# A sliding-window attention and mixer kernel: its instruction order from a written-out list in place of a scheduler in the kernel, and loads and stores on two queues

## The chip, the cores and the metric

The kernel runs on one core of one Trainium2 chip. A core has five engines that run side by side: TensorE (PE) multiplies matrices into PSUM, VectorE (DVE), ScalarE (ACT) and GpSimd (POOL) work elementwise, and SyncE (SP) issues transfers. The metric is the device time in microseconds (us). A profile's span is the time from the first to the last event of the program in one profiled execution; it is a little shorter than the timed figure.

## The reference

Attention with a sliding window of 128 keys and 4 sink keys, over 4 batches, 8 heads, 768 positions, 64 dimensions a head; its output x (768 x 512 a batch) goes through a mixer:

```
scores = q @ k.T / sqrt(64);  keep = is_sink | in_window
a = softmax(where(keep, scores, -1e9));  x = a @ v
tok = w_tok @ (alpha1 * x + beta1)            # mixes the 768 positions
u   = x + lam * tok
out = u + lam * (relu((alpha2 * u + beta2) @ w_ch1) @ w_ch2)   # 512 -> 2048 -> 512
```

## The kernel before

Every batch passes the same stages. Positions are tiled by 128 (six row tiles), heads are taken in pairs, and matrix operands are fp16.

- **Attention.** q and k of a head pair are loaded (`load_qk`), cast to fp16 and transposed into `qkT` (`trans`; batches 0 and 1 on PE as `tp`, batches 2 and 3 by a DMA transpose on SP). `scores` makes `S` on PE, ACT takes the exponential into `E`, DVE or POOL masks it. `sinks` does the sink keys (`sk`, `es`), `fill_vs` their values (`vs`). `pv` multiplies `E` with v (`vfs`), and DVE divides by the row sum (`rec`, then `x`, L850 and L851). POOL and DVE make `xh` = lam * (alpha1 * x + beta1) from it (`tm` L869, `xh` L872).
- **Token mix** (`tok`, L956): six products of 512 columns a row tile with the transposed `w_tok` (`wtokT`, made by `cast_wtok` at the start); DVE adds the result to x (L963), ACT or POOL casts it to `u` in fp16 (L356, L358).
- **Transpose of u** into `uT`: in batch 0 on PE (`uTp`, L997), else by DMA transpose on SP (L1015). DVE or ACT apply alpha2 and beta2 (L982, L980).
- **Channel mix.** First layer `mlp1`: four products of 384 columns for each of 16 feature tiles and two halves of the positions (`h`, L1036), relu on ACT (L1042) or DVE (L1044). Second layer: in batch 0 directly (`ch`, L1221), in batches 1 to 3 by a Strassen scheme of seven products (`P`, L1153), for which DVE makes sums of `hT` (`h_sums`: S3 L1094, S1 L1095, S2 L1096, S4 L1097) and of the weights (`w2_sums`, L1068), and DVE or POOL add the partial results to x (L1166, L1184, L1189, L1192). The row tile is then stored.

All of this is a list of some 1140 tasks. Each is added by `add` with a priority, the engines that may run it with an assumed cost in ns, the tasks it waits for and the buffers it uses:

```
a = add(p, {PE: 4 * 161}, mm, [done["uT", b, chk, c] for c in range(NC)] + [done["w1", fi // 4]], [ph, bu])
done["h", b, chk, fi] = add(p + 0.1, {ACT: 493, DVE: 556}, relu, [a], [ph, bh])
```

`Plan.run` is a list scheduler that runs while the program is built: it keeps a clock for each engine, a model of the transfer queues (`Rings`), and the buffers of each kind that are free (`homes`), and takes the open task that could start first, ties by priority; the priorities are shuffled by 30 seeds (`TURNS`). A POOL task, and a DVE task with `port=True`, also waits for the other's end (`port`). What it picks fixes three things: the order of the instructions on every engine, the engine of a task that has a choice, and which buffer a tile lives in (a later tile in the same buffer waits for the readers of the earlier one). It also puts idle products (`idle`, L349, on the tile `warm`) where PE would wait in the first 36 us. On the chip the order is fixed and nothing is assumed: an engine takes its instructions in turn and waits on semaphores. PSUM has four banks of kind `d` (all products but the scores) and two double ones of kind `S`.

SP issues nearly all loads, DMA transposes and stores (`nc.sync.dma_start`); POOL issues the loads that cast (w_ch1, and q and k of batch 0 except the first pair); ACT issues five small ones at the start. Tiny loads (`gate`) hold SP until parts of w_ch1 have landed.

Of the kernel before, what the change touches and what calls it, by code (L numbers as in the profile page):

```python
# [10 lines left out]
FP16 = mybir.dt.float16  # L11
# [6 lines left out]
SEEN = {PE: 200, ACT: 60, DVE: 60, POOL: 70}  # L18


class Buf:


    def __init__(self, kind, shape, dtype, name):
        self.kind, self.shape, self.dtype, self.name = kind, shape, dtype, name
        self.left = 0
        self.freed = 0.0
        self.home = None
        self.t = None


FW = 1.0

SWDONE = 1800.0


class Rings:


    WIRE = {"hw": 1600.0, "sw": 2100.0}  # L40

    HOLDS = 128.0

    def __init__(self):
        self.now = 0.0
        self.queue = {"hw": [], "sw": []}
        self.given = {"hw": [], "sw": []}

    def issue(self, ring, t, at):
        self.given[ring].append(t)  # L50
        self.queue[ring].append([t, float(t.lands[0]), float(t.lands[1]), at + self.WIRE[ring]])

    def room(self, ring, lands, at):

        keep = self.now, {r: [list(h) for h in q] for r, q in self.queue.items()}
        self.step(at)
        g = self.given[ring]
        last = g[-8] if len(g) >= 8 and g[-8].seen is None else None
        q = self.queue[ring]
        while last is not None and any(h[0] is last for h in q):  # L60
            self.step(float("inf"))
        over = sum(h[1] for h in q) + lands[0] - self.HOLDS
        while ring == "hw" and over > 0 and q:
            if q[0][1] < over:
                self.step(float("inf"))
                over = sum(h[1] for h in q) + lands[0] - self.HOLDS
            else:
                self.now += over * q[0][2]
                over = 0
        to = max(at, self.now)  # L70
        self.now, self.queue = keep
        return to

    def step(self, until):

        while True:
            heads = [(r, q[0]) for r, q in self.queue.items() if q]
            if not heads:
                return None
            live = [(r, h) for r, h in heads if h[3] <= self.now]  # L80
            later = [h[3] for r, h in heads if h[3] > self.now]
            turn = sum(h[2] for r, h in live)
            ends = [(self.now + h[1] * turn, r) for r, h in live]
            end = min(ends) if ends else (float("inf"), None)
            to = min([end[0], until] + later)
            for r, h in live:
                h[1] -= (to - self.now) / turn
            self.now = to
            if end[0] <= to:
                return self.queue[end[1]].pop(0)[0]  # L90
            if to >= until:
                return None

    def peek(self):

        keep = self.now, {r: [list(h) for h in q] for r, q in self.queue.items()}
        t = self.step(float("inf"))
        at = self.now if t else float("inf")
        self.now, self.queue = keep
        return at  # L100
# [11 lines left out]
class Plan:  # L112
# [19 lines left out]
    def run(self, prio):  # L132

        tasks = self.tasks
        rank = [0] * len(tasks)
        for r, i in enumerate(sorted(range(len(tasks)), key=lambda i: (prio[i], i))):
            rank[i] = r
        waiting = [len(t.needs) for t in tasks]
        ready = [t.since for t in tasks]
        homes = {k: [0.0] * n for k, n in self.homes.items()}  # L140
        busy = {k: [False] * n for k, n in self.homes.items()}
        for t in tasks:
            t.seen = None
            for b in t.uses:
                b.left, b.freed, b.home = 0, 0.0, None
        for t in tasks:
            for b in t.uses:
                b.left += 1
        free = {PE: 0.0, ACT: 3500.0, DVE: 3200.0, POOL: 500.0, SP: 0.0}
        rings = Rings()  # L150
        open_ = []
        steps = []

        def end(t, seen):
            t.seen = seen
            for b in t.uses:
                b.left -= 1
                b.freed = max(b.freed, seen)
                if b.left == 0:
                    busy[b.kind][b.home] = False  # L160
                    homes[b.kind][b.home] = b.freed
            for o in t.then:
                ready[o.i] = max(ready[o.i], seen)
                waiting[o.i] -= 1
                if not waiting[o.i]:
                    bisect.insort(open_, (rank[o.i], o.i))

        def pick():
            best = None
            spare = {k: sorted(h for h, x in zip(homes[k], busy[k]) if not x) for k in homes}  # L170
            for r, i in open_:
                at = ready[i]
                if best is not None and at > best[0]:
                    continue
                t = tasks[i]
                asked = {}
                for b in t.uses:
                    if b.home is None:
                        asked[b.kind] = asked.get(b.kind, 0) + 1
                if any(len(spare[k]) < n for k, n in asked.items()):  # L180
                    continue
                at = max([at] + [spare[k][n - 1] for k, n in asked.items()])
                own = None
                for e in t.engs:
                    at_e = max(free[e], at)
                    if e == POOL or (e == DVE and t.port):
                        at_e = max(at_e, port)
                    key = (at_e + FW * t.engs[e], at_e, r, at_e + t.engs[e], i, e)
                    if own is None or key < own:
                        own = key  # L190
                if best is None or own[1:] < best:
                    best = own[1:]
            return best

        open_ = sorted((rank[t.i], t.i) for t in tasks if not waiting[t.i])
        mode = None
        port = 0.0
        landing = float("inf")
        until, _, took = self.fill
        while len(steps) < len(tasks):  # L200
            best = pick()
            if best is None or landing <= best[0]:
                assert landing < float("inf"), "no task can go on"
                t = rings.step(float("inf"))
                end(t, rings.now + (SWDONE if POOL in t.engs else 300.0))
                landing = rings.peek()
                continue
            start, r, _, i, e = best
            open_.pop(bisect.bisect_left(open_, (r, i)))
            t = tasks[i]  # L210
            for b in t.uses:
                if b.home is None:
                    b.home = min((h, n) for n, (h, x) in enumerate(zip(homes[b.kind], busy[b.kind]))
                                 if not x)[1]
                    busy[b.kind][b.home] = True
            idle = None
            n = int((start - max(free[PE], 400.0)) / (took if free[PE] > 4500.0 else 110.0))
            if e == PE and free[PE] < until and n > 0:
                spare = [(h, k) for k, (h, x) in enumerate(zip(homes["d"], busy["d"])) if not x]
                if spare and min(spare)[0] <= free[PE]:  # L220
                    idle = (min(spare)[1], n)
                    homes["d"][idle[0]] = start
                    mode = None
            cost = t.engs[e]
            if t.lands:
                cost += rings.room("sw" if e == POOL else "hw", t.lands, start) - start
            if e == PE:
                if start < 4500.0:
                    cost = cost * 2
                if t.mode != mode:  # L230
                    cost = cost + 95
                mode = t.mode
            free[e] = start + cost
            if e == POOL or (e == DVE and t.port):
                port = free[e]
            steps.append((t, e, start, free[e], idle))
            if t.lands:
                rings.step(start)
                rings.issue("sw" if e == POOL else "hw", t, free[e])
                landing = rings.peek()  # L240
            else:
                end(t, free[e] + SEEN[e])
# [1187 lines left out]
```

The softmax here doesn't subtract the row's maximum and nothing guards it: scores larger than these inputs give would overflow.

## Time and profile before

| | |
|---|---|
| time, median of 3 | 256.93 us (256.84 to 257.47) |
| span of the profiled execution | 255.3 us |
| PE, DVE, ACT, POOL busy | 247.4, 190.0, 142.6, 88.3 us |
| instructions on PE, DVE, ACT, POOL | 2174, 402, 236, 108 |
| first `tok` product starts | 30.35 us |
| last product starts, last store issued | about 251.9, 252.46 us |
| moved from and to HBM | 29.91 MB read, 6.29 MB written |

The profile lists groups of instructions by source line, engine and tile. In a timeline a row has the start, the length, the engine, the line, what is written from what, how many instructions follow each other, and in brackets how long the engine was idle before it and who released it. A PE row's length runs to the end of its last product, and products overlap, so their distance is read from start to start. A `q` behind an engine's name (SPq, ACTq) is its sequencer, which issues transfers.

### The profile page before, as it was taken

Reading aid. Unit: us, or ns where it says so; the run is one execution under the profiler, and the core shown is the slowest. Engines: PE = TensorE matmul, PEld = TensorE weight load, DVE = VectorE, ACT = ScalarE, POOL = GpSimd, SP = SyncE. Lnnn points to the kernel's source line nnn. Section 1 sums busy time; section 2 is a strip of 40 time slices with the busy share of each in tenths; the row PEclk is TensorE's granted clock in tenths of the full one; section 3 lists DMA queues with packets and bytes.
Section 4 is the critical chain, followed back from the end, with each engine's and each line's share of the span. In section 5 each row is a group of like instructions: output and inputs, shape, how many; then the busy total and the mean of one; then the engine's idle time right before and its main releaser. Section 6 shows DMA issues by size and latency. Waiting matters only on the chain.

```text
span 255.3 us, 5519 instructions
## 1 busy us (share of the span) xinstructions
PE 247.4 (97%) x2174; PEld 160.9 (63%) x2174; DVE 190.0 (74%) x402; ACT 142.6 (56%) x236; POOL 88.3 (35%) x108
## 2 busy tenths in 40 slices
PE   8999998999999999899999999999999999999994
PEld 7754645675555544456678676558668666667883
DVE  6777998696878878578889997877789764136782
ACT  2689845989848035688971225867571125775000
POOL 7409802344445330159653460735310101000000
PEclk9999999999999999999999999999999999999999
DMA  6998999999943998599778689501000156000105
GB/s 202 195 223 292 216 230 392 373 370 218 218 73 115 186 260 190 117 205 220 155 138 182 125 191 251 85 3 21 3 0 3 59 167 146 0 0 3 63 4 185
DMA packets 86130, 38.80 MB, mean 152 GB/s; under 512 B 73540, under 2 KB 80460, under 8 KB 86104
## 3 DMA queue, kind: packets, MB, share of 16 engines
q1 hardware_dynamic: 82320, 35.14, 56.5%
q0 software_dynamic: 3744, 3.28, 8.1%
q8 instruction: 17, 0.28, 0.5%
q14 instruction: 9, 0.07, 0.1%
q10 hardware_dynamic: 40, 0.03, 0.0%
HBM read 29.91 MB, written 6.29 MB: 142 GB/s over the span
## 4 chain that ended last, share of the span: by engine, by line
PE 88%; DMA 4%; DVE 3%; POOL 1%; issue 1%; ACT 1%; POOLq 0%; ACTq 0%
PE h L1036 33%; PE P L1153 21%; PE tok L956 11%; PE ch L1221 8%; PE pv L825 5%; PE S L724 4%; DMA n<-in_q_dram 4%; DVE uT L982 1%; PE S L719 1%; PE tp L614 1%; PE pv L818 1%; POOL n L497 1%; PE wT L916 1%; ACT uT L980 1%; DVE w2f L1068 1%
## 5 line engine op out<-in xcount | busy, mean ns | idle before, releaser
L1036 PE MATMUL h<-uT,w1f 128*128 128x384 f16 x512 | 91.9, 326 | 2.7 <-DVE uT L982 1.3
L1036 PEld LDWEIGHTS <-w1f 128*128 128x128 f16 x512 | 47.3, 98 | 34.5 <-issue 5.5
L1042 ACT ACTIVATE hT<-h 128x384 f16<-128x384 f32 x99 | 48.3, 492 | 26.1 <-PE h L1036 25.6
L1153 PEld LDWEIGHTS <-hT 128*128 128x128 f16 x408 | 39.8, 98 | 6.7
L746 ACT ACTIVATE E<-S 128x1024 f16<-128x1024 f32 (+1 forms) x39 | 37.9, 1001 | 7.5 <-PE S L724 3.7
L869 POOL TENSOR_TENSOR tm<-x,la_b 128x512 f32<-128x512 f32 x18 | 26.2, 1454 | 26.3 <-DVE xh L872 19.1
L956 PE MATMUL tok<-xh,wtokT 128*128 128x512 f16 x144 | 33.4, 379 | 0.0
L356 ACT CAST u<-x 128x512 f16<-128x512 f32 x19 | 11.7, 618 | 31.2 <-DVE x L963 31.1
L1153 PE MATMUL P<-w2f,hT 128*128 128x256 f16 x216 | 25.9, 273 | 0.0
L1166 DVE TENSOR_TENSOR x<-x,P 128x256 f32<-128x256 f32 x45 | 18.3, 418 | 8.2 <-PE P L1153 7.9
L1044 DVE TENSOR_SCALAR hT<-h 128x384 f16<-128x384 f32 x29 | 15.8, 553 | 10.9 <-PE h L1036 10.5
L956 PEld LDWEIGHTS <-wtokT 128*128 128x128 f16 x144 | 14.0, 98 | 14.6
L1221 PE MATMUL ch<-w2f,hT 128*128 128x512 f16 x96 | 23.0, 379 | 0.0
L1153 PE MATMUL P<-w2s,hT 128*128 128x256 f16 x192 | 22.8, 273 | 0.0
L851 DVE TENSOR_TENSOR x<-pv,rec 128x256 f32<-128x256 f32 x48 | 20.4, 424 | 1.7
L358 POOL CAST vfs<-vnat 128x512 f16<-128x512 f32 x18 | 15.0, 840 | 16.2 <-DMA vnat<-in_v_dram 16.0
L963 DVE TENSOR_TENSOR x<-x,tok 128x512 f32<-128x512 f32 x24 | 16.2, 684 | 5.7 <-PE tok L956 5.7
L356 ACT CAST n<-nat 128x768 f16<-128x768 f32 x16 | 13.2, 829 | 10.8 <-DMA nat<-in_q_dram 8.8
L825 PEld LDWEIGHTS <-E 128*128 128x128 f16 x328 | 15.2, 97 | 6.0 <-issue 1.6
L825 PE MATMUL pv<-vfs,E 128*128 128x65 f16 x328 | 17.9, 194 | 0.0
L358 POOL CAST u<-x 128x512 f16<-128x512 f32 x5 | 3.1, 621 | 34.8 <-DVE x L963 21.1
L1221 PEld LDWEIGHTS <-hT 128*128 128x128 f16 x96 | 8.6, 98 | 9.1 <-issue 0.2
(131 smaller groups left out, 327.4 us busy)
## 6 DMA issues: line engine op xcount, KB each, us to landing
out_dram<-x SPq DMA_DIRECT2D x21, 256.0 KB, 2.8
nat<-in_q_dram SPq DMA_DIRECT2D x13, 384.0 KB, 5.3
nat<-in_k_dram SPq DMA_DIRECT2D x13, 384.0 KB, 5.7
vnat<-in_v_dram SPq DMA_DIRECT2D x18, 256.0 KB, 5.2
wst_w<-in_moe_w_ch_dram SPq DMA_DIRECT2D x8, 512.0 KB, 7.4
wtn<-in_moe_w_tok_dram SPq DMA_DIRECT2D x6, 384.0 KB, 4.7
w1f<-in_moe_w_ch_dram POOLq DMA_DIRECT2D x4, 512.0 KB, 11.1
v<-in_v_dram SPq DMA_DIRECT2D x12, 128.0 KB, 6.4
```

The lines of the kernel that those rows point to most:

```text
L356: nc.scalar.copy(o, i)
L358: engine[e].tensor_copy(o, i)
L746: nc.scalar.activation(eT.t, pS.t[:, :, 0 : n * w].rearrange("p e (i w) -> p e i w", i=n), AF.Exp, scale=scale)
L825: nc.tensor.matmul(po.t[:, hl, :], eT.t[:, e_, off + i, c : c + P], vf[j][:, h, :], start=(r < 2 and n == 0), stop=(n == len(parts) - 1 an ...
L851: nc.vector.tensor_mul(bx.t[:, 4 * G : 4 * G + 4, :], po.t[:, :, 0:D], rec.t.to_broadcast([P, 4, D]))
L869: engine[e].tensor_mul(bt.t, bx.t.rearrange("p h d -> p (h d)"), la1_b)
L956: nc.tensor.matmul(pt.t, wtokT[:, si, ti * P : (ti + 1) * P], hs[si].t, start=(si == 0), stop=(si == NR - 1))
L1036: nc.tensor.matmul(ph.t, w1f[:, c, fi * P : (fi + 1) * P], bu.t[:, c, chk * NTOK : (chk + 1) * NTOK], start=(c == 0), stop=(c == NC - 1))
L1042: nc.scalar.activation(bh.t[:, fi, :], ph.t, AF.Relu)
L1153: nc.tensor.matmul(pc.t, hh[:, nt * P : (nt + 1) * P], w(fi), start=(first and n_ == 0), stop=(n_ == HF - 1), skip_group_check=True)
L1166: nc.vector.tensor_add(row(bx)[:, cols], row(bx)[:, cols], pc.t)
L1221: nc.tensor.matmul(pc.t, bh.t[:, fi, nt * P : (nt + 1) * P], w2f[:, fi, :], start=(fi == 0), stop=(fi == NF - 1))
```

## The change

The scheduler leaves the kernel. What it would choose is written out: `ORDER` (the tasks in the order of the program), `ENGINES` (the engine of each), `HOMES` (the buffer of each tile), `IDLES` (where idle products stand, and how many). They come from a search outside the kernel, over fixed orders, with other assumed costs (for an exponential 50 + 0.85 a column in place of 170 + 0.835, for a relu 395 on ACT and 480 on DVE in place of 493 and 556), and with the port of DVE and POOL given to whoever asked first. Loads of q, k, v, w_tok and w_ch2 and all stores of results may be issued from ACT as well as from SP; DMA transposes stay on SP. `gates` has a tile of its own.

```diff
-    def run(self, prio):
-        ...
-    def emit(self, turns):
-        prio = [t.prio for t in self.tasks]
-        for seed in turns:
-            prio = shuffle(prio, seed)
-        for t, e, start, stop, idle in self.run(prio):
-            t.at = (e, start, stop)
+    def emit(self, order, engines, homes, idles):
+        own = iter(homes)
+        for t in self.tasks:
+            for b in t.uses:
+                if b.home is None:
+                    b.home = int(next(own), 16)
+        fills = {i: (home, n) for i, home, n in idles}
+        for i in order:
+            t = self.tasks[i]
+            e = (ACT, DVE, PE, POOL, SP)[int(engines[i])]
+            idle = fills.get(i)
...
+    queue = {SP: nc.sync, ACT: nc.scalar}
...
-    gates = sb.tile([1, 32], FP16, tag="pt_1", bufs=1, name="gates")
+    gates = const.tile([1, 32], FP16, name="gates")
...
-    TURNS = (13523, 134113, ...)
+    ORDER = (26, 6, 9, 7, 11, 8, 10, 3, 18, 0, 1, 72, 19, 73, 15, ...)
+    ENGINES = ("3313134433443333444444444444444433334443131211211202021212021203030121211211211210200200" ...)
+    HOMES = ("23100237431101330030022023311032230023102103010110051014013521b0006220a41141110314003021" ...)
+    IDLES = ((73, 0, 44), (46, 0, 16), (49, 0, 26), (90, 2, 8), (61, 2, 1), (109, 3, 1), (68, 3, 1),
+        (111, 2, 2), (88, 2, 2), (166, 2, 2))
...
-            p, {SP: 550}, lambda e: nc.sync.dma_start(
+            p, {SP: 570, ACT: 560}, lambda e: queue[e].dma_start(
                 bf.t, v[b, :, r * P : (r + 1) * P, :].rearrange("h p d -> p h d")),
...
-            add(p, {SP: 480}, lambda e: nc.sync.dma_start(out[b, ti * P : (ti + 1) * P, cols], row(bx)[:, cols]),
+            add(p, {SP: 520, ACT: 550}, lambda e: queue[e].dma_start(out[b, ti * P : (ti + 1) * P, cols], row(bx)[:, cols]),
```

How many of each task stand on which engine, before and after (the others stay): relus on ACT 99 and 77, on DVE 29 and 51; casts of q and k on ACT 16 and 21, on POOL 8 and 3; products of w_ch2 with lam on DVE 15 and 8, on POOL 1 and 8; additions of lam * beta1 (`xh`) on DVE 17 and 13, on POOL 1 and 5; loads and stores issued by ACT behind its first five 0 and 36. The order on PE changes from end to end; the end of batch 0's token mix, for one, goes from `tok_4, tok_3, uTp, uTp, h` to `tok_4, tok_3, uTp, uTp, tok_5, h`, and idle products from 106 to 103.

## The prediction

> **What bounds the kernel now.** I read the page first: part 1 (busy time) and part 4 (the chain that ended last).
>
> ```profile
> span 255.3 us, 5519 instructions
> PE 247.4 (97%) x2174; PEld 160.9 (63%) x2174; DVE 190.0 (74%) x402; ACT 142.6 (56%) x236; POOL 88.3 (35%) x108
> PE 88%; DMA 4%; DVE 3%; POOL 1%; issue 1%; ACT 1%; POOLq 0%; ACTq 0%
> ```
>
> TensorE (PE) is busy 97% of the span and is 88% of the chain. The change adds and removes no arithmetic, so it can only win what PE doesn't spend on its products: the time before the first token mix (`tok`), the gaps after it, and the tail. The windows by 10 us show who is full in the head, before `tok` (columns: PE, PEld, DVE, ACT, POOL busy, then clock, DMA share, GB/s):
>
> ```profile
> 10.00:20.00 10.00, 9.84 (x144) 5.48 (x141) 8.08 (x19) 9.05 (x16) 1.40 (x2) 1.00 1.19 214
> 20.00:30.00 10.00, 10.00 (x143) 5.79 (x142) 8.04 (x26) 9.95 (x17) 9.69 (x14) 1.00 0.99 265
> ```
>
> From 10 to 30 us ScalarE (ACT) is full: the head is a queue of exponentials and copies on ACT. After that I read PE's timeline for gaps. The two large ones:
>
> ```profile
> 31.56 7.07 PE L956 MATMUL tok<-xh,wtokT 128*128 128x512 f16 x32
> 38.47 0.83 PE L997 MATMUL uTp<-iden,u 128*128 128x128 f16 x12
> 39.78 0.32 PE L1036 MATMUL h<-uT,w1f 128*128 128x384 f16 x1 [0.47 <-ACT uT L980]
> 40.29 0.71 PE L1036 MATMUL h<-uT,w1f 128*128 128x384 f16 x2 [0.19 <-DVE uT L982]
> 41.38 2.27 PE L1036 MATMUL h<-uT,w1f 128*128 128x384 f16 x13 [0.38 <-ACT uT L980]
> ...
> 97.71 4.05 PE L956 MATMUL tok<-xh,wtokT 128*128 128x512 f16 x18
> 102.83 2.49 PE L1036 MATMUL h<-uT,w1f 128*128 128x384 f16 x12 [1.07 <-DVE uT L982]
> ```
>
> Starts are at most 0.163 us apart for an `h` product, 0.216 for `tok`, 0.056 for a transpose when nothing waits. Gap A (batch 0): 12 transposes from 38.47 end their turn at 39.14, three `h` take 0.49, and the fourth starts at 41.38: 41.38-39.14-0.49 = 1.75 us lost. Gap B (batch 1): 18 `tok` from 97.71 fill until 101.60; `h` starts at 102.83 and loses about 0.4 more before 105.25, together 1.6 us. Single stalls: 0.25 us near 110.8 (for L851) and this one, 0.5 us:
>
> ```profile
> 178.79 1.05 PE L1153 MATMUL P<-w2f,hT 128*128 128x256 f16 x8
> 180.20 0.82 PE L1036 MATMUL h<-uT,w1f 128*128 128x384 f16 x4 [0.37 <-DVE x L1166]
> ```
>
> So 4.1 us of stall are all there is between 31 and 252 us.
>
> [...] busy 97%, yet the gaps above are worth more than the missing 3% suggests, hence start-to-start times. [...] the same POOL product L869 takes 1.26 to 1.92 us, the cast of v 0.61 to 1.77. [...] Here issue time is not small:
>
> ```profile
> 50.97 8.28 SPq L514 DMA_DIRECT2D vnat<-in_v_dram x4
> ```
>
> Four issues in 8.28 us: 2.07 each, where an unhindered one takes about 0.4 to 0.57.
>
> **The change part by part.** (1) Scheduler out, lists in: no device cost. The cost tables in the `add` calls only fed the search; also nothing. `gates` in its own tile removes a buffer wait of 16-byte loads: nothing, SP does not end the chain.
>
> (2) Head. The order on the engines tells: POOL now issues two casting loads before anything else (1.5 us earlier), ACT starts with the copy of `tp_0_1` instead of `tp_0_0`, which goes to DVE. On DVE stand one copy (0.95) and the cast of k (0.56) ahead of that; the old trace has k landing at 7.2, DVE free of masks about 7.1: copy to 8.1, cast to 8.7, six transposes to 9.3, ACT from 9.4, against 8.07 now. ACT's queue up to the last exponential (E_4_1): 4 copies of 0.79, 8 exponentials of 512 columns at 0.55, 7 of 1024 at 0.97, 2 sink ones at 0.55, casts and copies 2.6, 2 casts of w_tok at 0.95, one w_tok copy 0.8... together about 20.0, so 29.4; a third w_tok cast to 30.4, its transposes, and `tok` at 31.1. Now: 30.35 with a transpose of 0.33 still inside, that is 30.7. Head: about +0.5 (bounds -0.5, if the earlier loads help, and +1.5, if ACT idles 1 us on the way, as it does now).
>
> (3) Gap A. After: `tok_3`, uTp, uTp, `tok_5` (1.30 us), then `h`. DVE behind `tok_4`: one add 0.65, two L881 of 0.72, then two L982 of 0.43; they end 0 to 0.3 us after `tok_5`. Saved: 1.75-0.2 = 1.55.
>
> (4) Gap B. From the third `tok` of batch 1 to `h` PE had ch 0.86 + three tok 3.9 = 4.8 us; after it has two ch 1.72, S and sinks about 1.0, three tok 3.9 = 6.6. Needed, from the trace: 4.8 plus the 1.23 wait = 6.0. Saved: 1.5 of 1.6, with 0.4 us to spare.
>
> (5) Two queues. 36 issues move from SP to ACT, at about 0.51 (the small ones at its start take 0.27 to 0.58): +18 us of ACT. To pay for that 22 relus (0.49 there, 0.55 on DVE), 4 copies and 4 casts leave ACT, 5 casts come: net +7 on an engine with 112 us free. They sit between relus and exponentials; four PSUM banks of 0.65 us each let PE run on about 1 us beyond an evacuation, so an unblocked 0.5 costs nothing. What is queued behind a blocked one is relus, and PE waits for those.
>
> (6) DVE against POOL. DVE takes 22 relus, gives 7 w2 products (0.74) and 4 xh sums (0.73), 5 mixed others: about the same 190 us. POOL takes these at 1.27 each and reaches about 115 of 255: hidden as work[...].
>
> (7) New tight places, by the same sums: the batch-0 transposes have 0.3 us to spare, the first sink product of batch 1 0.1, `tok_2` of batch 3 0.4 (its last xh on DVE), and the second P4 of batch 3 comes 0.5 late behind L1095/L1096. I put these at 1.2 in all (bounds 0 and 4); they take the place of the two single stalls, 0.8. Net +0.4.
>
> (8) Tail. Now the last product starts at about 251.9, its add at 252.01, its 128 KB store is issued at 252.46. After, ACT issues x_2's half (waiting for the add before last), and behind it the 256 KB store of x_4, which takes 2.0 to 2.4 against 1.7: +0.45.
>
> Sum: 255.3+0.5-1.55-1.5+0.4+0.45 = 253.6. The median of the times is 1.6 above the span (256.93-255.3): 255.2 us.
>
> **The rivals.** R1, slower: ACT becomes the bound in stretches. For it: an issue on a filled queue takes 2.07 (mean above), and ACT would stand still with relus behind[...]. Three such issues cost 2.07-1.0 each: 255.2+3.3 = 258.5. R2, no change: the gaps close, but the head comes 1.5 late and the tight places take 2.2 instead of 1.2: 255.2+1.0+1.0 = 257.2, about 257.0. For it: in the head ACT is at 9.95 of 10. R3, faster still: the head comes even, and nothing tight slips: 255.2-0.5-1.2 = 253.5. For it: the last 40 us show no stall at all.
>
> **How the numbers follow.** Forecast 0.46, R3 0.20: faster 0.66. R2 0.14, R1 0.20. The unknown issue cost (0.4 to 2.07) and the tight places (0 to 4) set the upper end, 258.0, inside R1; the head at -0.5 and no slip give the lower end, 252.9. Outside are about 0.06 below and 0.13 above.
>
> **What would show it.** Right: `tok` first at 31 +- 0.7; no wait of `h` for L982's successor over 0.4 us after the transposes of batch 0 and at batch 1; last PE end at about 250, the last store 2.6 behind it. Wrong: PE waits for relus behind ACT's DMA issues, issue times on ACT of over 1 us, `tok` after 32, or many PE waits of 0.2 to 0.5 for DVE[...].

## The result and the profile after

The changed kernel takes 258.60 us (median of 4 runs, 258.32 to 259.39) where the kernel before takes 257.06 (4 runs, 256.84 to 257.47). The ratio is 1.0063, with a 95% interval from 1.0037 to 1.0089: slower by 0.6%. The forecast was 255.2, faster, with a range up to 258.0: the sign and the range were wrong. Five executions of three kernels below were in a slower state, over 1.5% above the fastest of the same kernel and at a lower granted clock, and their medians and ranges leave these out.

In the new file the names have other line numbers: `tok` L849, `uTp` L890, `h` L929, `S` L617, `sk` L549, the copies and casts L155 (ACT) and L157 (DVE, POOL), the copies of `uT` L873 (ACT) and L875 (DVE), the DMA transposes of q and k L523 and of u L908. (In the experiments on the order of before most of these are one lower, `uTp` L889 for example.)

The page of the changed kernel, span, busy times and the chain of waits:

```profile
span 256.9 us, 5512 instructions
PE 248.4 (97%) x2171; PEld 162.0 (63%) x2171; DVE 190.3 (74%) x403; ACT 130.0 (51%) x212; POOL 114.5 (45%) x133
PE 81%; DMA 11%; ACT 2%; DVE 1%; issue 1%; POOL 1%; SPq 1%; ACTq 0%; DVEq 0%
```

The busy times came as forecast (DVE the same, POOL about 115, ACT not full). What is new is in the last line: transfers are 11% of the chain, where they were 4%. That share, 28 us, is not the loss, but it says where to look: at waits for transfers. PE's timeline shows what is lost, first at seam A (gap A of the prediction; seam B is its gap B):

```profile
31.89 6.64 PE L849 MATMUL tok<-xh,wtokT 128*128 128x512 f16 x30
38.36 0.83 PE L890 MATMUL uTp<-iden,u 128*128 128x128 f16 x12
39.03 1.46 PE L849 MATMUL tok<-xh,wtokT 128*128 128x512 f16 x6
40.47 4.71 PE L929 MATMUL h<-uT,w1f 128*128 128x384 f16 x28
```

No bracket stands behind `h`: the token product between the transposes and `h` hides the copies of `uT`, and 1.75 us of loss have become about 0.3. But the first `tok` starts at 31.89. Further down PE's timeline (two stretches):

```profile
97.13 0.39 PE L617 MATMUL S<-qkT 64*128 64x256 f16 x4
98.58 0.39 PE L617 MATMUL S<-qkT 64*128 64x256 f16 x4 [1.07 <-DMA qkT<-n]
98.91 0.40 PE L549 MATMUL sk<-qkT,ks 128*32 128x512 f16 x4
...
101.41 2.75 PE L849 MATMUL tok<-xh,wtokT 128*128 128x512 f16 x12
104.38 2.76 PE L929 MATMUL h<-uT,w1f 128*128 128x384 f16 x16 [0.22 <-DVE uT L875]
...
113.43 0.82 PE L929 MATMUL h<-uT,w1f 128*128 128x384 f16 x4
115.93 2.27 PE L929 MATMUL h<-uT,w1f 128*128 128x384 f16 x13 [1.68 <-ACT uT L873]
```

Seam B (104.38) lost only 0.38 us. Two waits are new, and both are long. The first scores of batch 2 stop halfway for a DMA transpose of q or k: from 97.25, the start of the fourth product, to 98.58 is 1.33, less one step of 0.05, which is 1.28 us. The second half of `h` of batch 1 stops at 113.92 until 115.93, less one step of 0.16: 1.85 us.

All of the losses, from the start-to-start distances in the trace (the last column is the mended kernel of the experiments below, with all three places and the tail):

| place | before | after | mended |
|---|---|---|---|
| first `tok` starts (before with the one transpose still inside) | 30.35 (30.68) | 31.89 | 31.08 |
| seam A (uTp to `h`, batch 0) | 1.75 | 0.27 | 0.28 |
| transposes of batch 1, `vs` of batch 2 | 0 | 0.42 | 0.18 |
| first scores of batch 2 | 0 | 1.28 | 0 |
| seam B (`tok` to `h`, batch 1) | 1.60 | 0.38 | 0 |
| second half of `h`, batch 1 | 0.25 | 1.85 | 0 |
| batch 3 | 0.53 | 0 | 0 |
| sum between head and tail | 4.13 | 4.20 | 0.46 |
| start of the last add to the end of the span | 3.29 | 3.79 | 3.45 |
| span | 255.3 | 256.9 | 252.0 |

The change closed the seams it was meant to close and lost the same sum at two others; the head is 1.2 us longer and the tail 0.5. That is +1.8, against +1.6 in the spans.

**Where the two new waits come from.** SP's queue before the first of them (start, time of the issue):

```profile
81.11 0.52 SPq L407 DMA_DIRECT2D vnat<-in_v_dram  x1
81.68 0.86 SPq L401 DMA_DIRECT2D nat<-in_q_dram  x1
82.59 4.22 SPq L523 DMA_TRANSPOSE qkT<-n  x1
```

and the casts on ACT that the later transposes need:

```profile
85.72 0.83 ACT L155 CAST n<-nat 128x768 f16<-128x768 f32 x1 [5.19 <-DMA nat<-in_q_dram]
89.49 0.83 ACT L155 CAST n<-nat 128x768 f16<-128x768 f32 x1 [2.94 <-DMA nat<-in_q_dram]
```

A q load issued at 81.68 has landed only when the cast starts at 89.49, 7.8 us later, and one transpose behind the two loads takes 4.22 us to be issued instead of about 1.2. The last of the eight transposes lands at 98.54, and PE goes on at 98.58. For the second wait, SP again:

```profile
104.88 2.68 SPq L908 DMA_TRANSPOSE uT<-u  x2
107.61 0.88 SPq L407 DMA_DIRECT2D vnat<-in_v_dram  x1
108.58 1.61 SPq L908 DMA_TRANSPOSE uT<-u  x1
```

and ACT, which copies `uT` as soon as it is complete:

```profile
107.79 0.40 ACTq L401 DMA_DIRECT2D nat<-in_k_dram  x1
...
114.58 0.71 ACT L873 ACTIVATE uT<-uT,ab 128x384 f16<-128x384 f16 x1 [2.12 <-DMA uT<-u]
```

The last transpose of u stands behind a v load on its own queue and beside a k load that ACT issued. It is issued at 108.58 and waited for until 114.5: 5.9 us. The transposes of u whose landing the trace has take 2.4 to 2.9 us. One of the two loads came from each queue, so here the second queue didn't keep the transpose clear of the loads. How the transfers share their engines, these views do not show.

**The head.** DVE and ACT of the kernel before, then of the changed one:

```profile
8.70 0.56 DVE L358 CAST n<-nat 128x768 f16<-128x768 f32 x1
```

```profile
8.07 0.80 ACT L356 COPY qkT<-tp 128x768 f16<-128x768 f16 x1 [0.39 <-PE tp L614]
```

```profile
8.12 0.96 DVE L157 COPY qkT<-tp 128x768 f16<-128x768 f16 x1 [0.68 <-PE tp L507]
9.29 0.56 DVE L157 CAST n<-nat 128x768 f16<-128x768 f32 x1 [0.22 <-DMA nat<-in_k_dram]
```

```profile
10.46 0.80 ACT L155 COPY qkT<-tp 128x768 f16<-128x768 f16 x1 [5.05 <-PE tp L507]
```

The second row of the changed kernel's DVE is the cast of k, and its bracket names the transfer: k has landed only at about 9.27. In the kernel before the trace has it landing at 7.16. ACT starts at 10.46 and ends its last exponential at 30.31, 19.85 us later, of which it is busy for 18.8.

### The profile page after: what moved, and what is told of

Read it like the earlier page. It is cut to its first block, busy times and chain, and to the rows that moved or that the text cites. A ratio compares the mean times of both kernels' runs of the same rounds, so it can differ in the third digit from the quotient of the medians.

```text
span 256.9 us, 5512 instructions
## 1 busy us (share of the span) xinstructions
PE 248.4 (97%) x2171; PEld 162.0 (63%) x2171; DVE 190.3 (74%) x403; ACT 130.0 (51%) x212; POOL 114.5 (45%) x133
## 4 chain that ended last, share of the span: by engine, by line
PE 81%; DMA 11%; ACT 2%; DVE 1%; issue 1%; POOL 1%; SPq 1%; ACTq 0%; DVEq 0%
PE h L929 31%; PE P L1046 22%; PE tok L849 9%; DMA uT<-u 4%; PE pv L718 4%; PE S L617 3%; DMA nat<-in_k_dram 3%; PE ch L1114 3%; DMA vnat<-in_v_dram 2%; DMA qkT<-n 2%; PE S L612 1%; PE tp L507 1%; PE tp L504 1%; PE pv L711 1%; PE wT L809 1%
## 5 line engine op out<-in xcount | busy, mean ns | idle before, releaser
L929 PE MATMUL h<-uT,w1f 128*128 128x384 f16 x512 | 90.3, 326 | 1.9 <-ACT uT L873 1.7
L929 PEld LDWEIGHTS <-w1f 128*128 128x128 f16 x512 | 47.9, 98 | 33.5 <-issue 5.0
L935 ACT ACTIVATE hT<-h 128x384 f16<-128x384 f32 x77 | 36.0, 491 | 26.2 <-PE h L929 25.6
L937 DVE TENSOR_SCALAR hT<-h 128x384 f16<-128x384 f32 x51 | 27.9, 554 | 25.0 <-PE h L929 24.3
L1046 PEld LDWEIGHTS <-hT 128*128 128x128 f16 x408 | 39.4, 98 | 6.8 <-issue 0.2
L849 PE MATMUL tok<-xh,wtokT 128*128 128x512 f16 x144 | 33.2, 379 | 0.0
L762 POOL TENSOR_TENSOR tm<-x,la_b 128x512 f32<-128x512 f32 x18 | 24.6, 1365 | 16.4 <-DVE xh L765 9.0
L155 ACT CAST n<-nat 128x768 f16<-128x768 f32 x21 | 17.2, 831 | 16.1 <-DMA nat<-in_q_dram 8.7
L849 PEld LDWEIGHTS <-wtokT 128*128 128x128 f16 x144 | 13.9, 98 | 14.9 <-issue 0.2
L1085 POOL TENSOR_TENSOR x<-x,pt 128x512 f32<-128x512 f32 x3 | 4.2, 1411 | 40.4 <-issue 36.3
L155 ACT CAST u<-x 128x512 f16<-128x512 f32 x15 | 9.2, 617 | 24.8 <-DVE x L856 23.2
L157 POOL CAST u<-x 128x512 f16<-128x512 f32 x9 | 7.2, 795 | 27.1 <-DVE x L856 25.3
L579 POOL TENSOR_SCALAR_AFFINE_SELECT E<-E 128x512 f16<-128x512 f16 x18 | 12.3, 710 | 14.8 <-ACT E L639 14.8
```

The source lines that it names most:

```text
L155: nc.scalar.copy(o, i)
L762: engine[e].tensor_mul(bt.t, bx.t.rearrange("p h d -> p (h d)"), la1_b)
L849: nc.tensor.matmul(pt.t, wtokT[:, si, ti * P : (ti + 1) * P], hs[si].t, start=(si == 0), stop=(si == NR - 1))
L929: nc.tensor.matmul(ph.t, w1f[:, c, fi * P : (fi + 1) * P], bu.t[:, c, chk * NTOK : (chk + 1) * NTOK], start=(c == 0), stop=(c == NC - 1))
L935: nc.scalar.activation(bh.t[:, fi, :], ph.t, AF.Relu)
L937: nc.vector.tensor_scalar_max(bh.t[:, fi, :], ph.t, 0.0)
```

## The experiments

The theory: three late transfers cost the time (k in the head, a q load of batch 2, the last transpose of u of batch 1), each because of which transfer stands ahead of or beside it; the second queue as such costs little. The rivals: the waits only move on when one is taken away, or two queues at once are what slows the transposes. In the diffs `behind` takes a task out of the list and puts it right behind another: `(620, 38)` puts task 620 behind task 38. Nothing else moves. Times were taken in several sessions, so kernels are compared by their ratios to the kernel before, which ran beside them each time.

### One q load early

Task 620 is the q load of heads 6 and 7 of batch 2, task 38 the last 16-byte gate load on SP.

```diff
+    ORDER = behind(ORDER, ((620, 38),))
     plan.emit(ORDER, ENGINES, HOMES, IDLES)
```

> One load issue is moved: q of heads 6 and 7 of batch 2 (it landed at 89.4 us, 7.7 us after its issue at 81.68) is issued on SP right after the 16-byte gate load, at about 71 us, where SP then stands idle for 6 us. Theory (the late transposes of q and k, not the second queue as such, cost the 1.28 us in the first scores of batch 2): the cast of that q at 89.49 runs by 86.6, the last qkT transpose lands by about 96 instead of 98.54, the wait between the two halves of the scores is under 0.3 us, and 1.0 to 1.3 us are saved: 257.3 to 257.6. Rival (the wait only moves on: the u transposes behind it keep their times): the wait of h at the seam of batch 1 grows from 0.38 to about 1.6 and the time stays at 258.6 within 0.3.

Measured: 258.09 us (18 runs), ratio to before 1.0046 [1.0031, 1.0061]. On PE the scores of batch 2 run through:

```profile
97.74 0.61 PE L617 MATMUL S<-qkT 64*128 64x256 f16 x8
98.28 0.40 PE L549 MATMUL sk<-qkT,ks 128*32 128x512 f16 x4
...
115.16 0.65 PE L929 MATMUL h<-uT,w1f 128*128 128x384 f16 x3 [1.72 <-ACT uT L873]
```

The wait of 1.28 is gone, and seam B lost 0.20 instead of 0.38: it did not move on. But the last transpose landed at 97.63, not by 96, so it is gone by a narrow margin. The other wait stands unchanged (1.88). In time the gain isn't shown: 0.5 us between the medians, and the intervals of the two ratios overlap. In the profiled run 0.8 of the 1.28 came (span 256.1): the first transposes of batch 1 waited 0.80 where they had not waited, and `tok` started 0.14 later.

### Two loads away from the transposes of u

Task 627 (v load) goes behind 479 (the last transpose of u) on SP; task 880 (k load) goes forward on ACT, behind the exponential 656.

```diff
+    ORDER = behind(ORDER, ((627, 479), (880, 656),))
     plan.emit(ORDER, ENGINES, HOMES, IDLES)
```

> Two load issues are moved away from the last u transposes of batch 1: the v load on SP goes behind the last of them (was 107.61, ahead of it), the k load on ACT goes forward to about 101 us (was 107.79). Theory (the last u transpose landed at about 114.4, 5.8 us after its issue at 108.58, because it stood behind these two loads; its fellows take 2.4 to 2.9): it is issued by 107.8 and lands by 110.5, the 1.85 us stall of the second half of h of batch 1 shrinks to under 0.3, and the time falls by 1.5 to 1.8: 256.8 to 257.1. Rival (the transpose was late because its cast was late, u at 106.2, and the DMA engines are busy with other loads anyway): it lands no earlier than 112.5 and at most 0.7 us is saved, 257.9 or more.

Measured: 258.11 us (20 runs, 255.87 to 259.69), ratio 1.0037 [1.0016, 1.0058]. The second half of `h` of batch 1 no longer stops:

```profile
114.06 0.61 PE L617 MATMUL S<-qkT 64*128 64x256 f16 x8
114.60 4.72 PE L929 MATMUL h<-uT,w1f 128*128 128x384 f16 x28
```

The 1.85 us are gone from PE, as the theory said, though the cast of u is no earlier against PE than it was: the rival's late cast was not the cause. The last transpose was issued at 108.82 (the theory said by 107.8) and had landed by 113.50, when ACT copied it without a wait; the trace doesn't have the landing itself. The time did not fall by 1.5 to 1.8: 0.5 between the medians, and again the intervals overlap. In the profiled run `tok` started at 32.73 (PE paused 1.78 us, start to start, before the transposes of k, against 0.49, and lost 0.8 us more in two waits at 27 us), and the transposes of batch 1 waited 0.77.

### The head's loads

Tasks 9 and 8 are GpSimd's first casting loads, 3 its first small mask; 48 is the cast of k, 47 the copy of `tp_0_0`.

```diff
+    ORDER = behind(ORDER, ((9, 3), (8, 9), (47, 48),))
     plan.emit(ORDER, ENGINES, HOMES, IDLES)
```

> Head only: the two casting loads that GpSimd issues at 1.31 and 2.21 us go behind its small masks (about 2.5 and 3.3, as in the kernel before), and the cast of k stands ahead of the copy of tp_0_0 on VectorE. Theory (the head is 1.2 us longer because k lands at 9.27 instead of 7.16, delayed by those two loads, and ScalarE's queue of about 20 us starts only then): k lands at 7.2 to 7.6, ScalarE's first copy starts at about 9.6 instead of 10.46, the first tok at 31.0 to 31.2 instead of 31.89, and 0.7 to 0.9 us are saved: 257.7 to 257.9. Rival (the later casting loads, v and w_tok loads set the head): first tok at 31.6 or later, 258.4 or more.

Measured: 258.01 us (18 runs), ratio 1.0038 [1.0022, 1.0054], which again overlaps with that of the changed kernel; the profiled run was the quickest of them (256.35, span 254.5), so its span says nothing of the typical time. DVE in that run:

```profile
7.20 0.72 DVE L157 CAST n<-nat 128x768 f16<-128x768 f32 x1
```

The cast of k starts at 7.20 and `tok` at 30.86, 1.03 us earlier. Here are all profiles of kernels with this order:

| first casting loads issued at | k's cast starts | first `tok` starts |
|---|---|---|
| 1.31 and 2.21 us (four kernels) | 9.29, 9.44, 9.46, 10.07 | 31.89, 32.03, 32.73, 34.02 |
| 2.19 and 3.10 us (six kernels) | 7.20, 7.39, 7.50, 7.56, 7.81, 7.85 | 30.86, 30.93, 31.08, 31.06, 31.45, 31.43 |

(The order of cast and copy, moved with the loads, can't explain the first group: the bracket there names k's transfer.)

The same step added to the kernel before (its order written out, alone tasks 8 and 9 first of all):

```diff
-    ORDER = (27, 6, 5, 7, 8, 10, 9, 11,
+    ORDER = (8, 9, 27, 6, 5, 7, 10, 11,
...
```

> The order of the kernel before, written out; alone two casting loads of GpSimd are issued first of all (about 1.31 and 2.21 us instead of 2.47 and 3.35). Theory (they take the DMA engines from the k load issued at 1.72): k lands at 9 us or later instead of 7.16, its cast starts at 9.1 to 9.9 instead of 8.70, ScalarE idles until then, and the head and the time grow by 0.4 to 1.2: 257.3 to 258.1. Rival (k landed late in the changed kernel for another reason, the order of SP's loads): k lands by 7.6 and the time stays at 256.9 within 0.3.

Measured: 257.73 us (12 runs), ratio 1.0040 [1.0019, 1.0061]: slower by the 0.4% expected, 0.9 us. DVE in the profiled run:

```profile
8.93 0.62 DVE L157 CAST n<-nat 128x768 f16<-128x768 f32 x1 [0.47 <-DMA nat<-in_k_dram]
```

The trace has the landing of k, issued at 1.72 in both kernels: 8.90 here, 7.16 before. Nothing but the two casting loads was moved, so they are the cause of the late landing, by 1.7 us. What it costs depends on the order around it. In this order DVE came to the cast only at 8.70 anyway, so the cast is 0.2 later and `tok` starts at 30.35 as before. Where the 0.9 us in time come from, this profile doesn't show. In the changed order the cast waits for k, and `tok` follows it.

### One queue in the changed order

All 36 issues of ACT go to SP.

```diff
+    own = list(ENGINES)
+    for i in (177, 186, 170, 621,
...
+        own[i] = "4"
+    ENGINES = "".join(own)
     plan.emit(ORDER, ENGINES, HOMES, IDLES)
```

> All 36 loads and stores that the changed kernel issues on ScalarE are issued on SP, in the same written-out order; nothing else moves. Theory (the second queue itself helps or is neutral; what costs is which transfer stands ahead of which transpose): SP has 36 more issues of 0.4 to 2 us, transposes come later, ScalarE gains 18 us that nobody waits for; the time is the same or up to 3 us longer: 258.6 to 261.6. Rival (two queues at once are the cause: loads of the ACT queue run beside SP's transposes and slow them): the last transposes of batches 1 and 2 land in about 2.5 us and the time falls to 256 to 257.

Measured: 259.26 us (4 runs), ratio 1.0085 [1.0051, 1.0119], not told apart from the changed kernel and not faster. The wait in the second half of `h` is gone here. The v load still stands right ahead of the last transpose of u (issued at 110.16 and 110.69), but the k load now comes behind it, at 112.71, and ACT copies at 114.71 without a wait: 4.0 us at most, not 5.9. That points to the k load on the other queue, though the run changes more than this. The scores of batch 2 wait 1.85 us instead of 1.28. The head was the worst of all: k was cast at 10.07. PE stood from 8.46 to 10.69, and the windows of 1 us show a second loss behind that (columns: PE, PEld, DVE, ACT, POOL busy, then granted clock, DMA share, GB/s):

```profile
12.00:13.00 1.00, 1.00 (x10) 0.61 (x7) 0.80 (x1) 0.03 (x1) 1.00 (x3) 0.50 1.31 217
13.00:14.00 1.00, 1.00 (x8) 0.34 (x8) 0.00 (x0) 0.60 (x1) 1.00 (x2) 0.50 1.29 225
```

After 2.2 us without a product the granted clock was 0.50 from 11.36 to 14.78 (worked out from the windows: 0.68 in the one from 11, 0.61 in the one from 14, 0.50 between). So the late k cost more than its lateness here: 0.8 us more delay of the cast than in the changed kernel went with a `tok` 2.1 later. The rival's forecast, 256 to 257, did not come.

### All three places, and the tail

The three sets of moves together; then also task 1130, the 256 KB store of x_4, behind 1127, ahead of two half stores on ACT.

```diff
+    ORDER = behind(ORDER, ((620, 38), (627, 479), (880, 656), (9, 3), (8, 9), (47, 48),))
     plan.emit(ORDER, ENGINES, HOMES, IDLES)
```

> The three sets of moves at once: the q load of batch 2 early, the v and k loads away from the last u transposes of batch 1, the two casting loads behind the small masks and the k cast ahead of the tp_0_0 copy. Theory (head, first scores of batch 2 and second half of h of batch 1 are the whole of the loss, and independent): from the span of the changed kernel, 256.9, go 1.0 (head), 1.28 and 1.85: 252.8, and with 1.8 between span and time 254.6 us, that is 0.9% faster than the kernel before. Rival (the single gains hide one another or move to the seam of batch 1 and to the batch-1 transposes at 53 us): 256.5 or more.

Measured: 255.18 us (254.78 to 255.43, 4 runs), ratio 0.9940 [0.9925, 0.9955]. This difference is clear: from 1.0063 to 0.9940, about 3.2 us.

```diff
-    ORDER = behind(ORDER, ((620, 38), (627, 479), (880, 656), (9, 3), (8, 9), (47, 48),))
+    ORDER = behind(ORDER, ((620, 38), (627, 479), (880, 656), (9, 3), (8, 9), (47, 48), (1130, 1127),))
```

> The same moves, and in the tail the 256 KB store of x_4 on ScalarE ahead of the half stores of x_0 and x_2 (its data is ready first). Theory (the tail is 0.45 us longer because that large store is issued last on ScalarE): last landing 0.3 to 0.5 us sooner after the last product, 254.2 us. Rival (the last half store of x_1 on SP sets the end and its landing does not hang on the large store): same as with the three places alone, within 0.2.

Measured: 253.94 us (3 runs, 253.74 to 255.12), ratio 0.9906 [0.9879, 0.9933]: 0.9% faster than the kernel before, with the lowest median here, though its interval overlaps with those of the three places alone and of the next kernel. The page:

```profile
span 252.0 us, 5512 instructions
PE 247.3 (98%) x2171; PEld 161.9 (64%) x2171; DVE 189.2 (75%) x403; ACT 129.9 (52%) x212; POOL 114.5 (45%) x133
PE 98%; DVE 0%; issue 0%
```

The chain is TensorE from end to end; the transfers have left it. Seam B and the last transposes of u on PE:

```profile
95.99 0.61 PE L617 MATMUL S<-qkT 64*128 64x256 f16 x8
...
101.66 2.76 PE L929 MATMUL h<-uT,w1f 128*128 128x384 f16 x16
...
110.71 4.72 PE L929 MATMUL h<-uT,w1f 128*128 128x384 f16 x28
```

No bracket is left. The three places together give 3.2 us, where no single one gave a time clear of its interval; the profiles of the singles show the other waits still there (with the head's loads alone moved, 0.6 us in the scores of batch 2 and 1.5 in the second half of `h`). The tail's edit is worth 0.3 us in the profiles (3.7 us from the last add to the end of the span becomes 3.45; the last landing takes 1.86 instead of 2.16 us); in the times it isn't shown.

The profile with the three places had one long wait left, 0.9 us at the transposes of batch 1. DVE there, and in the next run:

```profile
50.32 1.39 DVE L961 TENSOR_TENSOR w2s<-w2f 128x512 f16<-128x512 f16 x1
```

```profile
50.23 0.45 DVE L961 TENSOR_TENSOR w2s<-w2f 128x512 f16<-128x512 f16 x1
```

In the first, GpSimd's w2 product runs from 50.17 to 51.43 and the same difference on DVE takes 0.94 longer, to 0.3 us behind the end of the product; in the second that product had started at 49.13. The difference is slow in the run in which it falls together with the product; what holds it up, the views do not show. In the first run the product had waited for a load, in the second for PE. So one more move, task 349 (that difference) ahead of two relus:

```diff
-    ORDER = behind(ORDER, ((620, 38), (627, 479), (880, 656), (9, 3), (8, 9), (47, 48), (1130, 1127),))
+    ORDER = behind(ORDER, ((620, 38), (627, 479), (880, 656), (9, 3), (8, 9), (47, 48), (1130, 1127), (349, 304),))
```

> The three places and the tail, and one VectorE task moved: the first w2 difference (w2s) of the third group goes ahead of two relus, so that it no longer meets GpSimd's w2 product at 50 us (in the run with three places alone VectorE's difference took 1.39 us there instead of 0.45, the relu behind it was late and the batch-1 transposes waited 0.74 us; in the next run the two missed each other and nothing was lost). Theory ([...]decided by when a load lands): no wait over 0.3 us at the batch-1 transposes, 254.0 to 254.5 us, steadier. Rival (the transposes wait for the cast on GpSimd anyway): as without it, 254.5 to 255.2.

Measured: 254.90 us (14 runs, 254.17 to 256.48), ratio 0.9924 [0.9906, 0.9943]: no gain, as the rival said. The profile has 0.58 us of wait there again, this time for GpSimd's cast. But the two engines had met again in front of that cast: GpSimd's product took 1.77 us (from 50.94) instead of 1.26, and another difference on VectorE, from 51.50, took 1.49. So this run doesn't tell the meeting from the cast.

### What seam A and the second queue are worth

On this last kernel: `tok_5` of batch 0 (task 232) back ahead of the transposes; and, apart from that, all 36 issues on SP as above.

```diff
-    ORDER = behind(ORDER, ((620, 38), (627, 479), (880, 656), (9, 3), (8, 9), (47, 48), (1130, 1127), (349, 304),))
+    ORDER = behind(ORDER, ((620, 38), (627, 479), (880, 656), (9, 3), (8, 9), (47, 48), (1130, 1127), (349, 304), (232, 226),))
```

> The same kernel, with the token product tok_5 of batch 0 put back ahead of the two groups of uTp transposes, as in the kernel before, where h then follows them at once. Theory (the token product in between is what hides the copies of uT, worth 1.5 us): h waits 1.2 to 1.7 us behind the transposes and the time grows by 1.2 to 1.7. Rival (other work has moved off VectorE at that spot, so the seam closes without it): it grows by under 0.5.

Measured: 255.51 us (4 runs), ratio 0.9948 [0.9929, 0.9966]. The seam is open again:

```profile
38.83 0.83 PE L890 MATMUL uTp<-iden,u 128*128 128x128 f16 x12
40.93 4.38 PE L929 MATMUL h<-uT,w1f 128*128 128x384 f16 x26 [1.27 <-ACT uT L873]
```

In the trace that is a loss of 1.43 us, as expected. In time the medians are 0.6 apart, half of the least expected, and the intervals overlap: the profiled run had no wait at the transposes of batch 1 and started `tok` 0.37 earlier, so its span is the same, 253.7. The gain of the seam is shown in the traces, not in the times.

> The same kernel with all 36 issues of ScalarE on SP, order unchanged. Theory (with the order mended the second queue is worth little: it saves issue time on SP and lets two loads of batch 2 start earlier): 0 to 1.5 us longer. Rival (the second queue is a burden, its loads run beside transposes): up to 1 us shorter.

Measured: 255.93 us (6 runs), ratio 0.9950 [0.9929, 0.9970]. With one queue the scores of batch 2 wait 0.70 us again. The medians are 1 us apart (254.90 with two queues), but the intervals overlap and the two spans are alike (253.8 and 253.7): a gain from the second queue isn't shown.

### The second queue without the new order

The order of the kernel before, written out, and alone the 36 issues on ACT (shown as a statement; in the kernel these digits of `ENGINES` are changed):

```diff
+    own = list(ENGINES)
+    for i in (177, 186, 170, 621,
...
+        own[i] = "0"
+    ENGINES = "".join(own)
     plan.emit(ORDER, ENGINES, HOMES, IDLES)
```

> The order, engines and homes are those of the kernel before, written out; alone the same 36 loads and stores go to the queue of ScalarE. Theory (the second queue as such is neutral; the order of loads and transposes is what costs): 256.9 within 0.6. Rival (a second queue costs by itself, since its loads run beside the transposes of SP and slow them): 258 or more, with transposes of 4 to 6 us. Second rival (the second queue is what closes the seams): 255.5 or less.

Measured: 265.85 us (4 runs), ratio 1.0354 [1.0334, 1.0374]: 9 us slower. The theory failed; the first rival named only a lower bound, 258, and its mechanism is not what cost most. ACT and PE:

```profile
42.11 0.41 ACTq L443 DMA_DIRECT2D wst_w<-in_moe_w_ch_dram  x1
42.56 1.14 ACT L155 CAST u<-x 128x512 f16<-128x512 f32 x2 [5.35 <-DMA wst_w<-in_moe_w_ch_dram]
```

```profile
43.24 1.25 PE L889 MATMUL uTp<-iden,u 128*128 128x128 f16 x10 [4.00 <-ACT u L155]
```

ACT stands idle for 5.35 us until a w2 load has landed; the load that it issues and two casts of u come only then, and PE waits 4.00 us for those. Then the clock, in windows of 2 us (columns as above):

```profile
42.00:44.00 2.00, 0.76 (x8) 0.77 (x9) 0.00 (x0) 1.14 (x2) 0.00 (x0) 0.50 1.06 376
...
50.00:52.00 2.00, 2.00 (x14) 1.11 (x12) 2.00 (x5) 0.84 (x2) 0.00 (x0) 0.62 1.18 372
52.00:54.00 2.00, 2.00 (x18) 1.35 (x17) 1.26 (x3) 2.00 (x5) 0.00 (x0) 1.00 0.87 287
```

From 41.27 to 51.51 us the granted clock was 0.50 (worked out from the windows, 0.82 in the one from 40 and 0.62 in the one from 50). The sum: head 0.5, pause 4.15, seam A 0.85 longer, half clock about 2.5 (13 `h` at 0.32 instead of 0.163, and some transposes), 1.0 near 120 us: 9.0 of the 9.1 between the spans. First test, that one load (task 186) back on SP:

```diff
     for i in (177, 186, 170, 621,
...
         own[i] = "0"
+    own[186] = "4"
```

> The order of the kernel before with 35 of the 36 issues on ScalarE: the one w2 load at which ScalarE stood 5.35 us (issued at 42.11, with two casts of u behind it) is back on SP. Theory (that one issue, waiting in ScalarE's queue ahead of the casts, made 4.0 us of pause on TensorE, which then ran at half clock for about 10 us; together nearly all of the 9 us): 257 to 258.5 us, granted clock 1.00. Rival (the many issues together cost ScalarE its time): 262 or more.

Measured: 264.17 us (4 runs), ratio 1.0279 [1.0221, 1.0338]. The theory failed as it stood, and the number is the rival's (262 or more); but the pause had only moved to the next issue on ACT:

```profile
42.25 0.41 ACTq L396 DMA_DIRECT2D nat<-in_q_dram  x1
42.78 0.67 ACT L872 ACTIVATE uT<-uTp,ab 128x384 f16<-128x384 f16 x1 [5.35 <-DMA wst_w<-in_moe_w_ch_dram]
```

ACT is again idle for 5.35 us until a w2 load has landed, and what comes then is the issue of a q load, which has nothing to do with that one. What ties the two together, the views do not show. So three issues of that stretch back on SP (186, 170, 177):

```diff
-    own[186] = "4"
+    for i in (186, 170, 177):
+        own[i] = "4"
```

> The order of the kernel before with 33 of the 36 issues on ScalarE: the w2 load and two loads of batch 1 that stand between the first uT copies are back on SP. Theory ([...]TensorE pauses over 4 us and then runs at half clock): no pause over 1 us at the first uTp transposes, clock 1.00 throughout, 257 to 258.5 us. Rival (36 issues cost ScalarE its time everywhere): 262 or more.

Measured: 257.94 us (4 runs), ratio 1.0050 [1.0031, 1.0068], granted clock 1.00, seam A as in the kernel before (1.75). The one stretch was nearly all of it, and the rival (36 issues cost ACT its time everywhere) is out. With the other 33 issues on ACT about 1.3 us stay, of which 1.1 is a longer wait at 110 to 113 us. Here the trace fits the first rival of the run with all 36 issues, that a second queue's loads run beside the transposes and slow them:

```profile
102.97 3.83 SPq L907 DMA_TRANSPOSE uT<-u  x3
105.54 1.05 ACTq L406 DMA_DIRECT2D vnat<-in_v_dram  x2
110.76 0.38 DVE L874 TENSOR_SCALAR uT<-uT,ab 128x384 f16<-128x384 f16 x1 [1.09 <-DMA uT<-u]
```

The last of the three transposes of u is issued at 105.59, beside two v loads on ACT's queue, and its copy on DVE waits until 110.76; PE then waits 0.9 us for the x that stands behind that copy. In the kernel before all v loads follow on SP's own queue, from 107.28, and the same copy runs at 109.81 without a wait. With all 36 issues on ACT the trace has the landing too: 5.1 us (113.66 to 118.77). Nothing but the issuing engine was changed, so in these two runs loads issued on a second queue made a transpose late (5.1 us, and a copy 0.95 us later).

## Why the prediction was wrong, step by step

- **Head (2), the size was wrong.** +0.5 was forecast, +1.2 came. ACT's queue took 19.85 us against the 20.0 of the sum (the terms written there add to 20.75, and ACT was busy for 18.8, so that this agrees is partly luck). The term that failed is its start, 10.46 where the sum had 9.4. It rested on "the old trace has k landing at 7.2". The change moves two casting loads ahead of k's, and the prediction itself said so ("POOL now issues two casting loads before anything else"), but counted it only as a possible gain. k landed at about 9.27. The kernel before with nothing but these loads moved (8.90 instead of 7.16) shows the cause, and the six profiles with the later loads agree.
- **Seam A (3), right.** 0.27 is left of 1.75; undone, 1.43 us come back in the trace.
- **Seam B (4), nearly.** 0.38 left instead of 0.1. The 0.4 us to spare were used up: a cast of u on ACT stood behind a copy that waited 2.9 us for the same late transpose of q and k, and the transposes of u were issued behind it. With the q load early the profiles have 0 to 0.36 left, so this is only part of it.
- **Two queues (5), right on the issues, wrong to stop there.** The 36 issues on ACT took 0.34 to 1.03 us, and none was blocked by a transfer. But the sum put the transfers themselves at nothing, and a k load on ACT's queue stood beside the late transpose of u. That R1's figure, 258.5, is near the measured 258.6 is luck, since its mechanism isn't in the profile: PE waited for no relu behind an issue. It exists, as the order of before with two queues shows, in a form that the rival did not name: one issue on ACT, with two casts of u behind it, after 5.35 us of idle time that the landing of a w2 load ended. That a full queue made SP's four issues 2.07 us long was an estimate; the views show only the length.
- **VectorE and GpSimd (6), right on the busy times.** Where a product on GpSimd and a difference on VectorE ran at the same time, the difference took 1.39 us instead of 0.45, and PE lost up to 0.9 us in that run.
- **New tight places (7), the step that turned the sign.** The named places held: batch 0's transposes lost 0.14, the first sink product of batch 1, `tok_2` and the second P4 of batch 3 nothing. 3.1 us were lost at two that it did not name. The sums followed each place back through engines only. Both new waits run through transfers: load, cast, DMA transpose, copy. The prediction took transfers from the old trace as if they kept their times, though their order changed, and for 36 of them the queue. The bounds of 0 to 4 did hold the 3.5 us that were lost there.
- **Tail (8), right.** +0.45 forecast, +0.5 measured; with the large store moved forward about 0.3 come back.
- **The signs** it listed for wrong (late `tok`, slow issues on ACT, relus) were those of its rivals; `h` or `S` waiting for a DMA transpose was not among them.

With the head at +1.2, step 7 at +3.5 and seam B at -1.2, the prediction's own sum gives 255.3 + 1.2 - 1.5 - 1.2 + 3.5 - 0.8 + 0.5 = 257.0 of span. Measured: 256.9. Part (1), that the lists alone cost nothing, was not run alone; the order of before, written out with two loads moved, starts `tok` at 30.35 and loses 1.75 and 1.6 us at the seams, as the kernel before does. What stays open is the scatter: the time of these orders spreads more from run to run (255.87 to 259.69 over 20 runs with the two loads moved) than that of the kernel before (256.45 to 257.82 over 55), and a single profile can't say which of the late transfers does it each time.

## What to carry to other kernels

When a change reorders transfers, don't take their landings from the old trace: follow every chain of load, cast, DMA transpose and copy to the product that ends it, and note which loads stand ahead or in flight. Keep the first transfer that an engine waits for ahead of all others (k landed at 8.90 us instead of 7.16 with two loads moved ahead), and bulk loads away from transposes that are due, on whichever queue they are issued (5.9 and 5.1 us here, against 2.4 to 2.9). Issue a transfer on an engine that computes only where it need not wait there: in the order of before with two queues ACT stood for 5.35 us at one issue, and two casts of u with it.

## What the runs showed of the hardware

- Two pauses of TensorE were followed by a granted clock of 0.50: after 2.2 us without a product (8.46 to 10.69, the changed order with one queue) from 11.36 to 14.78; after 4.0 us (39.23 to 43.24, the order of before with all 36 issues on ACT) from 41.27 to 51.51, where 13 `h` were 0.32 us apart instead of 0.163. After pauses of 1.3 us (with the q load early) and 1.6 us (with the two loads aside) between 8.4 and 10.1 us it was 1.00 in every window up to 15 us.
- Where the changed kernel's trace has the landing, a DMA transpose of u takes 2.4 to 2.9 us. With a v load ahead and a k load beside it one took 5.9 there; in the order of before with all 36 issues on ACT one took 5.1. One of q or k took 4.22 us to be issued behind two loads, where the median of all 16 is 1.28.
- In the order of before with 36 and with 35 issues on ACT, ACT stood idle for 5.35 us until a w2 load had landed, around its own issue of another load at 42.11 and 42.25.
- Two casting loads issued 0.4 us before and 0.5 us after a k load on another queue delayed its landing by 1.7 us, with nothing else moved (7.16 in the kernel before, 8.90 in its order with these loads first).
